# First-microsecond DMA order in a gated attention mix: two weight pieces on ScalarE's queue, and SyncE's later weights arranged around x

## Chip, core and metric

One core of one Trainium2 chip. The metric is the device time of one execution in microseconds (us), median of several runs. The time runs about 1.7 us above the profiled span. Differences in this study are a few tenths of a per cent, so most kernels were timed in five rounds next to the kernel before, on the same chip. "k=1" and so on is a quarter of the contraction dimension (2 of 8 tiles of 128 rows). "Half 0" and "half 1" are two sets of 512 output columns.

## The reference, cut to what matters

```python
def reference(A_x, A_wqkv, A_wo, B_x, B_wqkv, B_wo, gate_w):
    x = A_x                                            # [1, 2048, 1024] bf16
    g = sigmoid((x * gate_w).sum(-1, keepdims=True))
    a = A_ref(x, A_wqkv, A_wo)                         # linear attention, 32 heads
    b = B_ref(x, B_wqkv, B_wo)                         # sliding window, dilated, softmax
    return g * a + (1 - g) * b
# inside A_ref (cut): qkv = x @ wqkv; q, k, v = split(qkv); pk = phi(k)
```

The change touches only the start of the first stage, `k = x @ wqkv[:, D:2D]` of block A.

## The kernel before

TensorE first runs 34 small warm-up matmuls on a tile of ones. It then computes K for four blocks of 128 rows at once, one quarter of the contraction after the other, in eight PSUM banks (the memory that TensorE adds up in). It can start when the first x piece (transposed by the DMA) and the first weight piece have landed.

```python
    load_wk(nc.scalar, 0, 0)              # weights of quarter k=0, half 0: ScalarE's queue
    with tc.manual_schedule(engines={SP}):
        load_xT(0, 0, 2)                  # x, k=0, row blocks 0 and 1 (transposing DMA, L94)
        load_xT(0, 2, 4)                  # x, k=0, row blocks 2 and 3
        load_wk(nc.sync, 0, 1)            # weights, k=0, half 1 (L98, 256 KB)
        for k in range(1, 4):
            load_xT(k, 0, 4)
            load_wk(nc.sync, k, 0)
            load_wk(nc.sync, k, 1)
        for t in range(4, NB):            # then the rest of x, row block by row block
            nc.sync.dma_start_transpose(out=xT[:, :, t * P:(t + 1) * P], ...)
    ...                                   # cut
            warm_up(34)
            first = [bank_k(i) for i in range(8)]
            for k in range(4):
                for half in range(2):
                    for t in range(4):
                        for kt in (2 * k, 2 * k + 1):
                            project(first[4 * half + t], t, kt, half)   # L168
                        if k == 3:
                            phi(work, pk[:, t, half * 512:(half + 1) * 512], first[4 * half + t])
            # then t = 4 .. 15; then the G stage (L219), and all the rest
```

## Time and profile before

| | kernel before |
|---|---|
| median before the prediction (3 runs) | 474.15 us (474.14 to 475.01) |
| median with 3 more runs, taken beside the changed kernel | 474.49 us (474.14 to 475.10) |
| the profiled run itself | 475.14 us, span 473.4 us |
| first K matmul / 17th (first of k=1) / first of G | 4.74 / 10.33 / 62.1 us |

The profile's table of busy time, one line: busy us, share of the span, instructions.

```profile
...
PE 466.0 (98%) x5731; PEld 244.6 (52%) x5762; DVE 277.7 (59%) x602; ACT 169.0 (36%) x272; POOL 15.3 (3%) x30
...
```

After the first ten microseconds TensorE's list of waits has nothing over 0.2 us. The waits in the whole run (us in total, times, longest):

```profile
PE pk_ps L168 <- DMA WkA<-in_A_wqkv_dram: 1.5, 1, 1.5
PE warm L174 <- DVE onesb L165: 1.1, 1, 1.1
...
```

The chain of work that ended last, in order of time (start, duration, what), shows which piece that wait is for. It is the weight DMA that SyncE issued at 5.36 us, and matmuls run from 10.33 us on.

```profile
...
4.07 1.24 SPq L94
5.32 0.05 issue
5.36 4.93 DMA WkA<-in_A_wqkv_dram
10.29 0.04 issue
10.33 1.67 PE pk_ps L168 x7
...
```

The next view gives the busy time of the K matmuls alone in stretches of 2 us. The columns are: stretch, its length, busy time and (x) how many matmuls lie in it or reach into it, granted clock, DMA share, GB/s. At full rate a stretch counts 11 (one start per 0.216 us, plus those that reach over its edges), at low clock 6. Some records are missing from a trace: here the 16th matmul's, due at 8.69 us.

```profile
4.00:6.00 2.00, 1.26 (x4) 1.00 0.83 170
6.00:8.00 2.00, 2.00 (x10) 1.00 1.15 227
8.00:10.00 2.00, 0.85 (x4) 1.00 1.50 227
10.00:12.00 2.00, 1.67 (x8) 1.00 0.79 178
```

The stretch from 8 to 10 us is half empty: that is the wait. The first four matmuls start 0.40 to 0.43 us apart and the rest 0.216 us apart. The full clock is recorded from 6.20 us. The clock column (the 1.00 before the DMA share) doesn't show that; only the spacing does.

### The profile page before, as it was taken

What the parts mean: (1) busy time and instruction counts of PE and PEld (TensorE: products, weight loads), DVE (VectorE), ACT (ScalarE), POOL (GpSimd) and SP (SyncE); (2) the same over time, 40 slices, a digit from 0 to 9 for tenths busy, and PEclk for the clock granted to TensorE, in tenths of its full rate; (3) what the DMA queues carried; (4) which work ended last, traced back from release to release, by engine and by line L of the source; (5) the groups of instructions that cost most, each with busy time, mean ns of one, the idle gap of its engine ahead of it and who ended that gap; (6) DMA issues with size and microseconds to landing.
All of it is one profiled execution on the core that took longest, in us unless ns stands there. A gap on an engine that the chain in (4) does not pass through costs nothing.

```text
span 473.4 us, 13138 instructions
## 1 busy us (share of the span) xinstructions
PE 466.0 (98%) x5731; PEld 244.6 (52%) x5762; DVE 277.7 (59%) x602; ACT 169.0 (36%) x272; POOL 15.3 (3%) x30
## 2 busy tenths in 40 slices
PE   7999999999999999999999999999999999999997
PEld 5444444444444444445666666666664444444444
DVE  0496689991329999999567676767560049800000
ACT  1343321102443333333555555555551134221122
POOL 2300000500000000000000000000000000000000
PEclk9999999999999999999999999999999999999999
DMA  8999980000644233627327455442663923221111
GB/s 168 231 225 381 349 269 0 0 1 0 204 133 111 96 137 126 161 96 241 106 57 101 81 85 94 102 91 51 91 167 73 200 90 78 68 55 45 35 34 45
DMA packets 98780, 55.40 MB, mean 117 GB/s; under 512 B 70178, under 2 KB 90658, under 8 KB 98722
## 3 DMA queue, kind: packets, MB, share of 16 engines
q1 hardware_dynamic: 93554, 50.10, 42.3%
q10 hardware_dynamic: 5168, 4.46, 2.9%
q8 instruction: 45, 0.74, 0.7%
q14 instruction: 13, 0.11, 0.1%
HBM read 26.10 MB, written 15.86 MB: 89 GB/s over the span
## 4 chain that ended last, share of the span: by engine, by line
PE 97%; DMA 1%; SPq 1%; issue 0%; ACT 0%
PE q_ps L387 26%; PE d_ps L584 12%; PE p_ps L294 12%; PE g_ps L219 12%; PE e_ps L584 11%; PE pk_ps L168 11%; PE p_ps L330 9%; PE po L466 2%; PE s2b L444 2%; DMA WkA<-in_A_wqkv_dram 1%; SPq L94 1%; PE kv_ps L239 0%; PE w_ps L282 0%; SPq L98 0%; ACT osb L589 0%
## 5 line engine op out<-in xcount | busy, mean ns | idle before, releaser
L387 PE MATMUL q_ps<-xT,WqB 64*64 64x512 bf16 x1024 | 68.3, 377 | 0.0
L387 PE MATMUL q_ps<-xT,WkB 64*64 64x512 bf16 x1024 | 67.9, 377 | 0.0
L153 DVE TENSOR_SCALAR e<-e 128x512 f32<-128x512 f32 x64 | 27.1, 423 | 64.5 <-ACT e L152 64.5
L294 PE MATMUL p_ps<-WvB,xT 128*128 128x512 bf16 x250 | 57.3, 379 | 0.5 <-issue 0.3
L168 PE MATMUL pk_ps<-WkA,xT 128*128 128x512 bf16 x251 | 55.9, 383 | 1.7 <-DMA WkA<-in_A_wqkv_dram 1.5
L219 PE MATMUL g_ps<-pk,xrow 128*128 128x512 bf16 x251 | 55.2, 379 | 0.3
L449 ACT ACTIVATE PT<-s2b 128x928 bf16<-128x928 f32 (+4 forms) x40 | 34.1, 854 | 45.6 <-PE s2b L444 45.6
L451 DVE TENSOR_TENSOR PT<-PT,mask 128x928 bf16<-128x928 bf16 (+4 forms) x40 | 23.6, 590 | 37.8 <-ACT PT L449 37.8
L330 PE MATMUL p_ps<-WqA,xT 128*128 128x512 bf16 x187 | 43.1, 379 | 0.3
L168 PEld LDWEIGHTS <-xT 128*128 128x128 bf16 x256 | 25.1, 99 | 32.0 <-issue 2.5
L584 PEld LDWEIGHTS <-pqT 128*128 128x128 bf16 x272 | 26.0, 98 | 29.8 <-issue 0.4
L584 PEld LDWEIGHTS <-OBT 128*128 128x128 bf16 x272 | 26.0, 98 | 29.4
L219 PEld LDWEIGHTS <-xrow 128*128 128x128 bf16 x256 | 25.1, 98 | 30.2
L294 PEld LDWEIGHTS <-xT 128*128 128x128 bf16 x256 | 24.6, 98 | 30.0 <-issue 0.9
L387 PEld LDWEIGHTS <-WkB 64*64 64x64 bf16 x1024 | 31.8, 107 | 15.4 <-issue 0.4
L387 PEld LDWEIGHTS <-WqB 64*64 64x64 bf16 x1024 | 31.5, 106 | 15.5 <-issue 0.9
L152 ACT ACTIVATE e<-pk_ps 128x512 f32<-128x512 f32 x32 | 18.9, 597 | 42.0 <-PE pk_ps L168 36.6
L299 ACT CAST tmp<-p_ps 128x512 bf16<-128x512 f32 x32 | 18.7, 589 | 37.6 <-PE p_ps L294 31.2
L584 PE MATMUL d_ps<-WoA,pqT 128*128 128x512 bf16 (+1 forms) x133 | 30.7, 370 | 0.2
L584 PE MATMUL d_ps<-WoB,OBT 128*128 128x512 bf16 (+1 forms) x134 | 30.7, 370 | 0.1
L330 PEld LDWEIGHTS <-xT 128*128 128x128 bf16 x192 | 18.8, 98 | 22.7
L584 PE MATMUL e_ps<-WoB,OBT 128*128 128x512 bf16 (+2 forms) x133 | 29.7, 363 | 0.2
(62 smaller groups left out, 484.1 us busy)
## 6 DMA issues: line engine op xcount, KB each, us to landing
vd<-tmp SPq DMA_DIRECT2D x16, 264.0 KB
xrow<-in_A_x_dram SPq DMA_DIRECT2D x4, 1024.0 KB
out_dram<-osb ACTq DMA_DIRECT2D x31, 128.0 KB
pqd<-tmp SPq DMA_DIRECT2D x12, 256.0 KB
WvA<-in_A_wqkv_dram SPq DMA_DIRECT2D x2, 1024.0 KB
WoA<-in_A_wo_dram SPq DMA_DIRECT2D x2, 1024.0 KB
WvB<-in_B_wqkv_dram SPq DMA_DIRECT2D x2, 1024.0 KB
WqA<-in_A_wqkv_dram SPq DMA_DIRECT2D x2, 1024.0 KB
```

What stands on the lines that cost most here:

```text
L152: nc.scalar.activation(out=e[:], in_=pj[:], func=ACT.Exp)
L153: nc.vector.tensor_scalar(out=e[:], in0=e[:], scalar1=1.0, scalar2=1e-6, op0=ALU.min, op1=ALU.add)
L168: nc.tensor.matmul(pj[:], lhsT=xT[:, kt, t * P:(t + 1) * P], rhs=WkA[half][:, kt, :], start=(kt == 0), stop=(kt == KT - 1))
L219: nc.tensor.matmul(pj[:], lhsT=xrow[:, t, kt * P:(kt + 1) * P], rhs=pk[:, t, half * 512:(half + 1) * 512], start=(t == 0), stop=(t == NB - 1))
L294: nc.tensor.matmul(st["pj"][:], lhsT=xT[:, kt, t * P:(t + 1) * P], rhs=WvB[half][:, kt, :], start=(kt == 0), stop=(kt == KT - 1))
L299: nc.scalar.copy(out=v[:, half * 16:(half + 1) * 16, 0:Dh], in_=st["pj"][:].rearrange("p (h e) -> p h e", h=16))
L330: nc.tensor.matmul(st["pj"][:], lhsT=xT[:, kt, t * P:(t + 1) * P], rhs=WqA[half][:, kt, :], start=(kt == 0), stop=(kt == KT - 1))
L387: nc.tensor.matmul(banks[o][64 * j:64 * j + 64, :], lhsT=lhsT(r, kt, j), rhs=rhs(r, kt), start=first and kt == 0, stop=kt == KT - 1, skip_ ...
L444: nc.tensor.matmul(s2b[64 * par:64 * par + 64, pair, :, o:o + w], lhsT=kts[c][r, par, k0:k0 + 64], rhs=qz[r, :, par, q0 % 512:q0 % 512 + w ...
L449: nc.scalar.activation(out=pt[:, :, 0:W_], in_=s2b[:].rearrange("p a b s -> p (a b) s")[:, :, 0:W_], func=ACT.Exp, scale=SCALE)
L451: nc.vector.tensor_tensor(out=pt[:, :, 0:W_], in0=pt[:, :, 0:W_], in1=mask[:, None, base:base + W_].broadcast_to([P, 4, W_]), op=ALU.mult)
L584: nc.tensor.matmul(st["ps"][:, 0:n], lhsT=lhsT, rhs=W[c0 // 512][:, c, c0 % 512:c0 % 512 + n], start=(side == 0 and c == 0), stop=(side == ...
```

## The change

Its intent: take one 256 KB weight piece off SyncE's queue in front of x of k=1, and put one of the two weight pieces of each later quarter ahead of its x piece, so that TensorE finds the second quarter ready.

```diff
     load_wk(nc.scalar, 0, 0)
+    load_wk(nc.scalar, 0, 1)
     with tc.manual_schedule(engines={SP}):
         load_xT(0, 0, 2)
         load_xT(0, 2, 4)
-        load_wk(nc.sync, 0, 1)
         for k in range(1, 4):
+            load_wk(nc.sync, k, 0)
             load_xT(k, 0, 4)
-            load_wk(nc.sync, k, 0)
             load_wk(nc.sync, k, 1)
```

The instruction streams of TensorE, VectorE and GpSimd are the same in both kernels. ScalarE has one DMA issue more, SyncE one less.

## The prediction

> **What bounds the kernel now.** TensorE. The profile's busy table gives PE 466.0 of 473.4 us (98%), and the chain of waits is 97% PE. PE's waits list has one DMA wait in the run: 1.5 us for WkA. The timeline shows where it is: the first matmul of the K projection starts at 4.74 us, the 16 matmuls of the first quarter (k=0) are done issuing by 8.7 us, and the next one starts at 10.33 us. From there PE runs at 0.216 us a matmul nearly without a gap to the end. So a microsecond won before 10.33 us should be one of the total; PE, DVE and POOL streams are unchanged.
>
> **What the change does.** A SyncE weight issue takes 0.47 to 0.60 us, an x transpose 1.23 to 1.3 us. By the trace's semaphore updates, pieces on SyncE's queue land in issue order: slot 3 (issued 3.44) at 6.98, slot 4 (4.07, x of k=1) at 7.99, slot 5 (5.36) at 10.29, slot 6 (5.98) at 11.01, slot 7 (6.50, x of k=2) at 12.06, slots 8, 9 at 12.84, 13.56, slot 10 (x of k=3) at 14.54, slots 11, 12 at 15.30, 16.02. Before, slot 5 was the weights of k=1, half 0: PE waits for it until 10.29. After, these weights sit in slot 3 (6.98), and slot 5 is k=1, half 1. The x pieces of k=1 to 3 keep their slots.
>
> If the slots land as before, PE needs: k=1 at 8.7 (weights 6.98, x 7.99: no wait); k=1 half 1 at 10.4 (slot 5, 10.29: just in time); k=2 at 12.15 (x 12.06: just in time); k=3 at 15.6 (x 14.54). So at most 10.33 - 8.70 = 1.6 us is won.
>
> **What it costs.** k=0 half 1 moves to ScalarE's queue, issued at about 1.3 us, so its 256 KB (about 0.75 us of 16 engines at 47 ns a 1 KB packet) flow beside the first x piece, which lands at 4.70 and starts PE. The Trainium skill ("DMA: Bandwidth & Descriptors", "Issuing engines are not separate DMA queues") says that both queues run on the same 16 engines and interleave. The windows view gives a DMA share of 0.73 to 0.88 from 2 to 5 us, so some room; I estimate the first matmul is late by 0.2 to 0.5 us. Part is given back: PE runs at 0.43 us a matmul until 6.2 us, where the full clock is granted, so a late start loses only slow matmuls.
>
> Net gain about 1.3 us (0.3%).
>
> **Predicted time: 472.8 us**, 472.0 to 474.0 (8 in 10). Faster by over 2%: 0.01; within 2%: 0.98; slower by over 2%: 0.01.
>
> **What would show each step.** Right: PE's 1.5 us wait for WkA is gone or below 0.5 us; the first K matmul starts at 4.9 to 5.3 us; the 17th starts near 8.9 to 9.3 us; the G stage starts about 1.3 us earlier than 62.29; later stages keep their lengths. Wrong: a new wait of similar size at k=1 half 1, at x of k=2, or at the first x piece.
>
> **What would make it wrong.** Transposes of x stalling for over 1 us (256-byte packets begun at 9.24 us ended near 10.87) at another place, now where PE has no slack; the granted clock rising later because PE pauses between the warm-up matmuls and the first real one; run-to-run spread (474.14 to 475.01), which is as large as the gain.

## More of the kernel before

("Slow run" further down is this document's own word for a run over 475 us.)

## The result, and the profile after

| | before | after |
|---|---|---|
| median, 6 runs each | 474.49 us | 473.87 us |
| range | 474.14 to 475.10 | 473.68 to 474.32 |
| first K matmul / 17th / first of G | 4.74 / 10.33 / 62.1 us | 5.62 / 9.08 / 60.9 us |

The ratio of the fast runs is 0.9988, with a 95% interval from 0.9975 to 1.0000. It is the mean time of one kernel's fast runs over that of the other's of the same rounds, so not quite the ratio of the medians. The interval just reaches 1: this set alone hardly shows a gain.

TensorE's waits after. The wait for weights is gone, and another has come in front of the very first matmul:

```profile
PE warm L174 <- DVE onesb L165: 1.1, 1, 1.1
PE pk_ps L168 <- DMA xT<-in_A_x_dram: 0.8, 1, 0.8
```

The chain after. The first x piece, issued at 0.80 us as before, now reports its landing only at 5.57 us, and no other DMA is in the chain up to 12 us:

```profile
...
0.80 4.77 DMA xT<-in_A_x_dram
5.57 0.04 issue
5.62 6.43 PE pk_ps L168 x29
```

The same stretches as before, for the K matmuls alone. The first stretch has nearly none, then the rate is full without a hole:

```profile
4.00:6.00 2.00, 0.39 (x2) 1.00 1.02 249
6.00:8.00 2.00, 2.00 (x11) 1.00 1.07 227
8.00:10.00 2.00, 2.00 (x11) 1.00 1.15 234
10.00:12.00 2.00, 2.00 (x11) 1.00 0.93 226
```

In these two profiles the difference is accounted for. Before, the first 16 matmuls took 5.59 us (10.33 - 4.74): 16 x 0.216 = 3.45 us of work, 0.71 us because the first four ran at low clock, and 1.43 us of waiting. After, they took 3.46 us. So 2.13 us are won and 0.88 us lost at the start, a net of 1.25 us. This is what the start of G shows (62.13 to 60.88), and from there to the end both runs take the same time (411.24 us). It is twice the difference of the medians: the profiled run of before was one of its slowest (475.14 us). The profiled run of after was an ordinary one (473.85 us), in which the full clock came early, at 4.48 us.

Landing times, read from the updates of each DMA's semaphore (the counter by which it reports) in the two traces (the last of its 16):

| piece on SyncE's queue | before: content, landed | after: content, landed |
|---|---|---|
| 1 | x k=0 blocks 0, 1: 4.70 | same: 5.57 |
| 2 | x k=0 blocks 2, 3: 5.30 | same: 5.94 |
| 3 | weights k=0 half 1: 6.98 | weights k=1 half 0: 7.04 |
| 4 | x k=1: 7.99 | x k=1: 7.96 |
| 5 | weights k=1 half 0: 10.29 | weights k=1 half 1: 10.07 |
| 6 | weights k=1 half 1: 11.01 | weights k=2 half 0: 10.77 |
| 7 | x k=2: 12.06 | x k=2: 11.84 |

In these two traces a place, from the third on, keeps its landing time within 0.25 us though another piece stands in it. Only the first two x pieces are later. Other traces are less regular: in four profiles with the DMA order of after, the fifth place landed between 9.44 and 10.13 us.

Why the first x piece is later can be seen in the DMA packets. The counts are per 0.1 us, taken from the packet records of the trace of after. q1 is SyncE's queue, q10 ScalarE's. The first x piece is 512 packets of 256 bytes. After each piece come 32 packets of 4 bytes, which I take for its report of completion:

```
from us   q1 256 B   q1 4 B   q10 1 KB
3.6          41         0         6
3.7          28         0        23
3.8          16         0        28
3.9           1         0        33
4.0           0         0        33
4.1           0         0        36
4.2           0         0        36
4.3           0         0        39
4.4          42        26         9
4.5          88         4         2
```

All 512 data packets of the first x piece have started by 3.9 us. From 4.0 to 4.4 us no packet of SyncE's queue starts, neither its completion packets nor the data of the second x piece. The second weight piece on ScalarE's queue has the engines to itself. When that piece is through, the completions follow. In the trace of before, with no such piece, they ran from 3.2 to 3.6 us. All six profiles with this piece issued at 1.30 us have the gap, of 0.52 us, begun at 3.66 to 3.91 us; those with no second piece on ScalarE's queue by then have none.

The Trainium skill ("DMA: Bandwidth & Descriptors", "Queues, rings and completion order") says that each engine takes turns between the queues that have work for it, and that a completion write lands only after all earlier writes of that engine, across queues. It adds that a turn lasts a whole packet in the page's own sense, typically 9 to 17 descriptors. An estimate: the weight piece is 256 transfers of 1 KB, 16 for each of 16 engines, and the trace has 0.046 us for one, so a single turn could hold 0.74 us of it. A gap of 0.52 us is within what this allows. But it isn't the whole: in the three kernels further down that hold the piece back to 2.29 us, SyncE's queue also starts nothing for 0.28 to 0.81 us, just after the first x piece has sent its 4-byte packets, while only 20 to 45 packets of ScalarE's piece start and on average 6 to 9 of the 16 engines are busy with them. The ordered completion write could account for the completions being late, but the second x piece's data stood still as well. The runs show the gap, not which rule makes it.

### The profile page after: what moved, and what is told of

Read it like the earlier page. It is cut to its first block, busy times and chain, and to the rows that moved or that the text cites. A ratio compares the mean times of both kernels' runs of the same rounds, so it can differ in the third digit from the quotient of the medians.

```text
span 472.1 us, 13169 instructions
## 1 busy us (share of the span) xinstructions
PE 467.1 (99%) x5762; PEld 244.3 (52%) x5762; DVE 277.8 (59%) x602; ACT 169.0 (36%) x272; POOL 15.4 (3%) x30
## 3 DMA queue, kind: packets, MB, share of 16 engines
q10 hardware_dynamic: 5440, 4.72, 3.1%
## 4 chain that ended last, share of the span: by engine, by line
PE 98%; DMA 1%; ACT 0%; issue 0%
PE q_ps L387 27%; PE d_ps L584 12%; PE p_ps L294 12%; PE pk_ps L168 12%; PE g_ps L219 12%; PE e_ps L584 12%; PE p_ps L330 9%; PE po L466 2%; PE s2b L444 2%; DMA xT<-in_A_x_dram 1%; PE kv_ps L239 0%; PE w_ps L282 0%; ACT osb L589 0%
## 5 line engine op out<-in xcount | busy, mean ns | idle before, releaser
L387 PE MATMUL q_ps<-xT,WqB 64*64 64x512 bf16 x1024 | 68.3, 377 | 0.0
L387 PE MATMUL q_ps<-xT,WkB 64*64 64x512 bf16 x1024 | 67.9, 377 | 0.0
L584 PEld LDWEIGHTS <-pqT 128*128 128x128 bf16 x272 | 26.0, 98 | 29.7 <-issue 0.4
L584 PEld LDWEIGHTS <-OBT 128*128 128x128 bf16 x272 | 26.0, 98 | 29.4
L387 PEld LDWEIGHTS <-WkB 64*64 64x64 bf16 x1024 | 31.7, 107 | 15.4 <-issue 0.4
L387 PEld LDWEIGHTS <-WqB 64*64 64x64 bf16 x1024 | 31.5, 106 | 15.6 <-issue 0.9
L584 PE MATMUL d_ps<-WoA,pqT 128*128 128x512 bf16 (+1 forms) x136 | 30.9, 370 | 0.0
L584 PE MATMUL d_ps<-WoB,OBT 128*128 128x512 bf16 (+1 forms) x136 | 30.8, 370 | 0.0
L584 PE MATMUL e_ps<-WoA,pqT 128*128 128x512 bf16 (+2 forms) x136 | 30.0, 363 | 0.0
```

The costliest lines, as they stand in the source:

```text
L387: nc.tensor.matmul(banks[o][64 * j:64 * j + 64, :], lhsT=lhsT(r, kt, j), rhs=rhs(r, kt), start=first and kt == 0, stop=kt == KT - 1, skip_ ...
L584: nc.tensor.matmul(st["ps"][:, 0:n], lhsT=lhsT, rhs=W[c0 // 512][:, c, c0 % 512:c0 % 512 + n], start=(side == 0 and c == 0), stop=(side == ...
```

## Experiments

Theory at the start: the gain is the removed wait, and the late first x piece is the price of the piece moved to ScalarE's queue. Rivals: the new arrangement around x is what helps; the lateness was chance or came from the order of issue. Twelve runs were made, of nine further kernels and three repeats, and all gave correct results. The medians of the kernel before, on the chips of the three sets, were 474.85, 474.82 and 474.93 us.

### The changed kernel again

No edit.

> The changed kernel once more, as the measure for the other runs and a second profile. My theory: the first K matmul waits for the first x piece again, starting at 5.2 to 5.7 us (4.74 in the profile of before), no wait for weights; the time at which the full clock is granted differs from run to run (6.2 us in the profile of before, 4.5 us in that of after), and G starts at 60.9 to 61.6 us. Median 473.9 us. Rival (the late first x piece was chance): the first matmul starts at 4.7 to 4.9 us.

Measured: median 474.73 us (473.65 to 476.29), ratio 0.9998 (0.9981 to 1.0014). The first matmul started at 5.82 us, so the late first x piece was no chance. But three of six runs took over 475 us. The profile is of the slowest one (476.29 us), and the same view of the K matmuls in stretches shows why:

```profile
4.00:6.00 2.00, 0.18 (x1) 1.00 1.03 227
6.00:8.00 2.00, 2.00 (x6) 1.00 1.10 247
8.00:10.00 2.00, 2.00 (x6) 1.00 1.25 251
10.00:12.00 2.00, 1.95 (x9) 1.00 1.00 261
```

Six matmuls in 2 us where the first profile had eleven: the array ran at low clock until 10.39 us, where the full clock is recorded. G started at 63.3 us, later than before. This was not foreseen in size: I had expected a clock that differs between 4.5 and 6.2 us.

The Trainium skill ("TensorE: Matmul & The Clock Gate", Part 1) says that the clock is raised after a busy activity window of about 3.4 us, and that this window runs freely, so that its phase differs from run to run. The 10.39 us fit this: one window earlier, 6.98 us, closes a window (3.57 to 6.98) in which TensorE had paused for 0.90 us between the last warm-up matmul and the first real one. That pause is new: in the kernel before, the warm-up led straight into the first matmul.

### The rearrangement alone

```diff
         load_xT(0, 2, 4)
+        load_wk(nc.sync, 0, 1)        # back on SyncE's queue (and off ScalarE's)
         for k in range(1, 4):
             load_wk(nc.sync, k, 0)    # as in the change
```

> Half 1 of the first weight quarter goes back to SyncE's queue, just after the first x pieces; the later weights stay arranged around their x piece. My theory: what counts is that one 256 KB piece leaves SyncE's queue, so here the first matmul starts at 4.7 us as before, but the x piece of k=1 is now the fifth piece of the queue and lands at 9.3 to 10.3 us, so that PE waits about 1 us for it: G starts at 61.6 to 62.2 us, median 474.4 us, as before. Rival (the arrangement of weights around x makes the gain): no such wait, 473.9 us or less.

Measured: median 474.19 us (473.84 to 474.54), ratio 0.9984 (0.9972 to 0.9996). The first matmul started at 4.63 us, as expected, and TensorE's waits in its profile were these (the warm-up's left out):

```profile
...
PE pk_ps L168 <- DMA xT<-in_A_x_dram: 0.8, 1, 0.8
...
PE pk_ps L168 <- DMA WkA<-in_A_wqkv_dram: 0.3, 1, 0.3
```

The wait for x of k=1 (landed 9.23 us) is there, as my theory said. Still, the time is better than before, against my number, and G started at 61.09 us, where I had expected 61.6 to 62.2. That is as early as in the two profiles of the changed kernel's faster runs (60.88 and 61.11 us). In both orders TensorE can start k=1 when the fifth piece of SyncE's queue has landed: here that is x, at 9.23 us; before it is a weight piece behind x, at 10.2 to 10.3 us in two profiles. Why the fifth place is sooner in this order isn't settled. One difference: in both profiles of before, x packets of 256 bytes begun from 9.2 us on stalled for over 1 us and ended at 10.8 to 10.9 us (the prediction names this), while here no packet begun before 12.8 us took over 0.6 us. One profile doesn't show whether that is the order's doing. In any case the rearrangement alone reached most of the gain, so my theory that only the piece leaving SyncE's queue counts did not hold.

### The move alone

```diff
         for k in range(1, 4):
-            load_wk(nc.sync, k, 0)
             load_xT(k, 0, 4)
+            load_wk(nc.sync, k, 0)
             load_wk(nc.sync, k, 1)
```

(relative to the changed kernel)

> Half 1 of the first quarter on ScalarE's queue as in the change, but SyncE issues x, then both weights of each later quarter, as before. My theory: the x piece of k=1 lands near 7.4 us, its weights near 8.0 us, PE has no wait for weights, the first x piece is late as after (first matmul 5.2 to 5.7 us), and the median is within 0.2 us of the changed kernel's, 473.9 us. Rival (the arrangement makes the gain): PE waits for the weights of k=1 past 9 us, 474.4 us.

Measured: median 474.03 us; six runs, four from 473.67 to 474.12 us, and two of 476.21 and 476.35 us. The ratio is 0.9995 (0.9976 to 1.0013). The profile, of a fast run, has one DMA wait, of 0.9 us, for the first x piece. The 17th matmul starts at 8.92 us without one listed, but only just: the weights of k=1 landed at 8.88 us, not at the 8.0 us that I expected. G started at 60.72 us. So the arrangement adds little once the piece is moved, and the slow runs came with the move: this kernel pauses 0.91 us before its first matmul as well, and the kernel with the rearrangement alone, which doesn't pause, had no run over 474.54 us.

### Holding the piece back: a first try

Three VectorE memsets of the tile's first quarter come ahead of the DMA that writes it, and the issue is moved down in the program to follow them.

```diff
-    load_wk(nc.scalar, 0, 1)
...
-            nc.vector.memset(onesb[:], 1.0)
+            nc.vector.memset(onesb[:], 1.0)
+            nc.vector.memset(WkA[1][:, 0:2, :], 0.0)    # three times
+            load_wk(nc.scalar, 0, 1)
```

> The changed kernel, with the issue of the second weight piece on ScalarE's queue held back from 1.3 us to about 2.8 us by three VectorE memsets of the tile that it writes. My theory: its packets then no longer run before the first x piece reports its landing; the first matmul starts at 4.7 to 4.9 us, the piece itself lands by 6.6 us, PE waits under 0.3 us for it, G starts at 60.0 to 60.9 us, and the median is 0.4 to 0.8 us below the changed kernel's. Rival (the first x piece is late for another reason, such as the order of issue on SyncE): the first matmul stays at 5.5 us and the time at 473.9 us.

Measured: 478.44 us, 0.7% slower than before (1.0056 to 1.0082). This was not the experiment I meant. The memsets ended at 2.92 us, but being later in the program, the DMA had been given the semaphore of the first x piece, and so was issued only after that had landed, at 4.56 us. The piece landed at 10.05 us. The longest of TensorE's waits in this profile is for it:

```profile
PE pk_ps L168 <- DMA WkA<-in_A_wqkv_dram: 2.3, 1, 2.3
...
```

It still taught two things. With nothing of ScalarE's queue behind the first weight piece, the first x piece landed at 4.48 us. And the pause of 2.3 us cost the clock: the records show it full from 7.10 us, half from 10.52 to 13.93 us, then full again, in steps of 3.41 us, which agrees with the skill's window.

### A longer warm-up

```diff
-            warm_up(34)
+            warm_up(44)
```

(relative to the changed kernel)

> The changed kernel with 44 warm-up matmuls in place of 34 (0.107 us each while the clock is low), so that TensorE is not idle for 0.9 us before the first x piece lands at 5.6 to 5.8 us. Theory: it is this pause that, in some runs, puts off the full clock by one window (10.4 us in the second profile of the changed kernel, against 4.5 in the first). Then no run is slow here: the full clock comes before 7.6 us in the profile, all runs lie within 473.4 to 474.5 us, median about 473.8 us, against 473.7 to 476.3 us with 34. Rival (the late clock comes from something else[...]): runs over 475 us stay, about one in four.

Measured: median 474.87 us (473.76 to 475.07), ratio 0.9994 (0.9980 to 1.0008). No run is in the 476 range, and the pause is gone from the profile, where the full clock is recorded at 6.91 us. But my range was wrong: three of five runs lie at 474.87 to 475.07 us. The profile (475.0 us) shows what I left out. The warm-up ran until the first matmul at 5.79 us, 0.3 us past the landing of the x piece (5.47), and a start at 5.79 with full clock at 6.91 leaves three slow matmuls. G started at 61.60 us, 0.72 us after the first profile of the changed kernel; another 0.40 us was lost after that, in a stage that is the same in all kernels (see "Why the prediction was right or wrong"). The longer warm-up gained no time here. One run of five, at 475.07 us, is over the 475 us of the rival, and five runs are too few to show that the slow ones are gone.

### The pause without the change

The kernel before, with a shorter warm-up:

```diff
-            warm_up(34)
+            warm_up(26)
```

> The kernel before with 26 warm-up matmuls in place of 34: TensorE idles from about 3.9 us to the first x piece at 4.7 us, a pause of 0.8 us without any of the change. Theory (the pause puts off the clock in some runs): some of the runs are slow by 1 to 2 us, over 476 us, where the full clock comes after 8 us; the others stay at 474.3 to 475.3 us. Rival (the pause costs nothing): all runs are as those of the kernel before, 474.3 to 475.4 us.

Measured: median 475.37 us (474.80 to 475.90), ratio 1.0012 (1.0000 to 1.0025). In the profile TensorE pauses 0.71 us before the first x piece, the full clock comes at 8.68 us, and the K matmuls run at half rate until then, as the view in stretches shows:

```profile
4.00:6.00 2.00, 1.22 (x3) 1.00 0.77 176
6.00:8.00 2.00, 2.00 (x6) 1.00 1.23 204
8.00:10.00 2.00, 2.00 (x9) 1.00 1.63 243
```

So in this profile the clock comes late after a pause, without any of the change. But the cost that I expected, over 476 us, did not come. The slow first matmuls filled the time in which the kernel before would have waited anyway: the 17th started at 10.43 us, 0.10 us after the 10.33 us of the profile of before, and G at 62.22 us, 0.09 us later. The removed wait had been a cushion.

### A double dose on ScalarE's queue

```diff
-    load_wk(nc.scalar, 0, 1)
+    load_wk(nc.scalar, 0, 1); load_wk(nc.scalar, 1, 0)    # and not on SyncE's queue
```

> A double dose: ScalarE's queue issues the first weights of k=1 (half 0) as well, right after the two pieces of the first quarter, and SyncE has one piece less before x of k=1. Theory (packets of ScalarE's queue put off the landing of the x pieces): the first x piece lands another 0.3 to 0.9 us later, at 5.9 to 6.5 us, the first matmul starts there, and the pause of TensorE grows to 1.2 to 1.8 us, so that most runs get the full clock late: median 474.5 to 476 us. Rival (the delay came from the order of issue alone): first matmul at 5.6 us as in the changed kernel.

Measured: median 474.40 us (474.20 to 474.56), ratio 0.9992 (0.9980 to 1.0005). My number for the first x piece was wrong: it landed at 5.80 us, as in the changed kernel (5.57 to 5.80 in its three profiles). The second x piece paid instead, landing at 6.80 us in place of 5.94 to 6.16. So more on ScalarE's queue did not delay the first x piece further. It fits better that an x piece is held up by the ScalarE piece that is moving when it would report: the third piece landed at 6.46 us, 0.34 us before the second x piece. The first matmul started at 5.85 us after a pause of 0.95 us, but no run was slow (the clock came at 4.75 us in the profiled one); my expectation of mostly slow runs failed.

### Holding the piece back, properly

```diff
-    load_wk(nc.scalar, 0, 1)
+    nc.vector.memset(WkA[1][:, 0:2, :], 0.0); nc.vector.memset(WkA[1][:, 0:2, :], 0.0)
+    load_wk(nc.scalar, 0, 1)
```

(in its old place in the program, so that it has a semaphore of its own)

> Again the changed kernel with the second weight piece on ScalarE's queue held back, now by two memsets of VectorE alone (in the run before, the piece had also got the semaphore of the first x piece, and so was issued only after that had landed, at 4.56 us). It is issued at about 2.3 us here in place of 1.3 us. Theory: the first x piece lands at 4.6 to 5.2 us in place of 5.6, since fewer of the piece's packets run before it reports; the first matmul starts by 5.2 us, a pause of under 0.6 us; the piece lands by 6.3 us; the wait for it is under 0.3 us; median 0 to 0.5 us below the changed kernel's fast runs (473.3 to 473.9 us). Rival: the first x piece lands at 5.5 us or later all the same.

Measured: median 474.09 us (473.74 to 474.42), ratio 0.9985 (0.9972 to 0.9997). The piece was issued at 2.29 us. The first x piece landed at 4.20 us, better than expected, and the first matmul started at 4.72 us without a pause. The piece landed at 6.11 us, and the *second* x piece right after it, at 6.54 us. TensorE's waits in this profile, the warm-up's left out:

```profile
...
PE pk_ps L168 <- DMA xT<-in_A_x_dram: 0.4, 1, 0.4
...
```

The chain of work that ended last now runs through the second x piece, issued at 2.15 us:

```profile
...
2.15 4.39 DMA xT<-in_A_x_dram
6.54 0.05 issue
6.59 2.55 PE pk_ps L168 x11
...
```

This confirms the cause by moving it: issue the ScalarE piece at 1.30 us and it is the first x piece that reports right after it (0.27 to 0.37 us after, in five profiles; 0.64 in the double dose); issue it at 2.29 us and it is the second, 0.43 to 0.45 us after it (this profile and the next two). One thing stays unexplained: the first x piece landed at 4.06 to 4.35 us in these three profiles, sooner than in those with no second piece on ScalarE's queue by then (4.48 to 4.74 us).

### Held back, with the matmuls in the order of landing

```diff
             for k in range(4):
+                for pair in ((0, 1), (2, 3)) if k == 0 else ((0, 1, 2, 3),):
                     for half in range(2):
-                        for t in range(4):
+                        for t in pair:
```

(relative to the kernel just above; one more run has 31 warm-up matmuls in place of 34)

> The kernel of the last set in which the second weight piece is issued at 2.3 us, and in which TensorE waited 0.4 us for the second x piece (landed 6.54, the weight piece 6.11). Here the matmuls of the first quarter are taken in another order: row blocks 0 and 1 with both halves of the weights, then row blocks 2 and 3, so that the weight piece is needed first and the second x piece after eight matmuls. Theory: that wait of 0.4 us goes, the second half of the quarter is done by 8.8 us or earlier, G starts at 60.4 to 60.9 us, the median is 0.2 to 0.5 us below that of the kernel before it (474.1), so 473.6 to 473.9, with no run over 474.6. Rival (the first microseconds are pinned by the landing of the next quarter, as in the kernel before): no gain, a new wait before the 17th matmul.

> The same with 31 warm-up matmuls in place of 34: in the last profile the first x piece had landed at 4.2 us, but TensorE was in the warm-up until 4.7. Theory: the first matmul starts at 4.4 to 4.7 us with no pause over 0.3 us, and the gain is 0 to 0.3 us beside 34 warm-ups. Rival (even a short pause puts off the full clock): one run or more slower by over 1 us.

Measured with 34: median 473.83 us (473.53 to 474.27), ratio 0.9976 (0.9964 to 0.9988). With 31: 473.68 us (473.39 to 474.12), ratio 0.9973 (0.9961 to 0.9985). The first matmul starts at 4.46 and 4.40 us. The wait for x is gone, but its place is taken by a wait for the weight piece, which I had not expected. From TensorE's waits in the profile with 31 warm-ups:

```profile
...
PE pk_ps L168 <- DMA WkA<-in_A_wqkv_dram: 0.5, 1, 0.5
...
```

With 34 it is 0.8 us, since the clock came at 4.17 us there and the first four matmuls were done sooner. The start of G, at 60.65 us with 34, lies where I expected it. The difference between the two warm-ups, and that to the kernel one step before, lie within their intervals. Both are faster than the kernel before: their intervals end at 0.9988 and 0.9985.

### The changed kernel a third time, and the kernel before a second profile

> The changed kernel a third time, beside the others of this set: it tells whether its slow runs come back (three of twelve so far took over 475 us). Theory: one or two of the five or six take over 475 us[...]; the rest 473.6 to 474.4. The first matmul starts at 5.4 to 5.9 us.

Measured: median 474.03 us (473.55 to 476.37), ratio 0.9987 (0.9969 to 1.0004), one slow run in six. The first matmul started at 5.84 us. The clock had been full since 3.80 us, and stayed so over a pause of 1.4 us.

> The kernel before, for a second profile: the only profile of it is of one of its slowest runs (475.14 us; median 474.5 to 474.9). Theory: the wait of TensorE for the first weights of k=1 ends at 9.7 to 10.4 us whatever the time of the full clock, G starts at 61.5 to 62.2 us.

Measured: one run of 475.04 us (state unknown). Here the array was at full rate from the first matmul on (4.66 us, starts 0.22 us apart), and it gained nothing. TensorE's waits in this run:

```profile
PE pk_ps L168 <- DMA WkA<-in_A_wqkv_dram: 2.0, 2, 1.6
...
```

And its chain of work that ended last, in order of time:

```profile
...
5.37 4.84 DMA WkA<-in_A_wqkv_dram
10.21 0.04 issue
10.25 1.89 PE pk_ps L168 x8
...
```

The same piece lands at 10.21 us (10.29 in the first profile), and G starts at 62.05 us (62.13). What the clock gave in the first quarter went into a longer wait. In these two runs the time of the kernel before is set by that landing, not by the clock.

### Pause and clock in all profiles

| kernel | pause before the first K matmul, us | full clock from, us |
|---|---|---|
| before | none | 6.20 |
| rearrangement alone | none | 4.46 |
| held back, first try | none | 7.10 |
| longer warm-up | none | 6.91 |
| held back; pairs; pairs with 31 | none | 5.62; 4.17; 5.52 |
| after, three profiles | 0.84; 0.90; 1.39 | 4.48; 10.39; 3.80 |
| move alone | 0.91 | 3.91 |
| double dose | 0.95 | 4.75 |
| before, 26 warm-ups | 0.71 | 8.68 |

The second profile of before is left out, since it has no clock record. The pauses are counted from the modelled end of the last warm-up matmul, as the view of waits does; counted from its start plus one spacing they are 0.16 to 0.21 us longer (0.91 us in the last row). Without a pause the clock comes anywhere from 4.2 to 7.1 us. With one it either comes before the first matmul (by 4.75 us) or after 8.6 us, and nothing lies between. The slow runs of the changed kernel are 4 of 18 (475.08 to 476.37 us), those with the move alone 2 of 6. The mark of 475 us was set by eye: the kernel before passes it in 12 of 37 runs, but never goes over 475.43 us. Only one of the slow runs was profiled (476.29 us), so that the others have the same cause is inferred from it, not seen.

## Why the prediction was right or wrong

The predicted time was 472.8 us (472.0 to 474.0); 473.87 us were measured. The class "within 2%" and the range held. The predicted gain of 1.35 us (474.15 to 472.8) was twice the 0.62 us between the medians.

- **What bounds the kernel: right.** TensorE is busy throughout, and the only DMA wait is the one at 10.33 us. A shift there was a shift of the whole run: 1.25 us at the start of G, and 1.3 us in the span (473.4 to 472.1).
- **The wait for WkA goes: right.** It isn't in any profile of the changed kernel. The places on SyncE's queue from the third on landed within 0.25 us of before in the first profile, and no new wait came at k=1 half 1 (10.07 us, needed at 10.80) or at x of k=2.
- **"I estimate the first matmul is late by 0.2 to 0.5 us": the step that failed.** It was late by 0.88, 1.08 and 1.10 us in the three profiles. I read the free DMA share as room to share. The traces show instead that SyncE's queue stood still for 0.52 us while the second weight piece moved, and an x piece whose data was through reported only after it.
- **"A late start loses only slow matmuls": wrong in some runs.** The pause that comes with the late start can put off the full clock by a whole window, as the second profile shows. I had named this as a risk without a weight.
- **The base: too low.** The three runs gave 474.15 us, six gave 474.49, and those of the later sets 474.8 to 474.9. The one profile was of a run of 475.14 us. I took a median from one run and the 1.5 us of wait from another. Why the runs of before differ by over 1 us among themselves isn't settled: in two profiles with quite different clocks G starts within 0.1 us. Both are of runs over 475 us. An estimate for the fastest run of before: 474.14 us less 1.72 us beside the span and 411.24 us after the start of G leaves 61.2 us for the start of G, so its wait may have been some 0.9 us shorter than the profiled one; no such run was profiled. Part of the spread lies elsewhere: from the start of G to the end the profiles take 411.14 to 411.73 us, and the difference is in the attention stage (first L387 to first L584 matmul, 141.18 to 141.76 us), which no edit touched. The start of G therefore tells more of the change than one run's time.
- **The size as a whole.** The agreement of the span (1.3 us) with the prediction is partly luck: the start was later than I put it (0.88 against 0.2 to 0.5 us), and the clock in that run came earlier (4.48 against 6.20 us), which saved the 0.71 us of slow matmuls. Over three sets, the 14 of 18 runs that weren't slow average 473.9 us, against 474.8 us for all 37 runs of before (474.14 to 475.43): 0.9 us, a sum that leaves out the worst runs on one side only. The four slow ones take half of that back (mean of all 18: 474.4 us).
- **The change as a bundle.** In the experiments I first gave the gain to the piece that leaves SyncE's queue. But G starts at 61.09 us with the rearrangement alone and at 60.72 us with the move alone (one profile each), against 60.88 and 61.11 us with both: either half does it, and they don't add up.

So where did the expected gain go? The old wait was 1.5 us of weights in the profiled run, and probably less in the faster runs of before. Of these 1.5 us, 0.9 to 1.1 came back as a first x piece that reports late, and now and then more is lost, in the one slow run that was profiled because the array starts with its clock low. The version that holds the piece back and takes the matmuls in the order of landing keeps the gain (473.68 us, ratio 0.9973 to before). The 15 runs of the three kernels that hold it back to 2.29 us had no slow one (all up to 474.42 us). In the last set the mean with 31 warm-ups is 0.6 us below that of the changed kernel, and most of that is the changed kernel's one slow run.

## What to carry to other kernels

At a cold start, ask not only how soon a transfer is issued but which transfer will be moving when the one that everybody waits for has to report its landing; a second queue can help the later pieces and hold up the first. If a kernel warms TensorE up before its data arrives, a change that moves the landing can open a pause in which the clock may come late; look at the warm-up again, but note that here making it longer closed the pause and gained no time. A wait that ends at a fixed time hides every loss and every gain in front of it, so take it out of the sum before judging what comes earlier.

## What the Trainium skill lacked or had wrong

- "DMA: Bandwidth & Descriptors", "Issuing engines are not separate DMA queues": it says that queues interleave; only another section ("Queues, rings and completion order") gives the grain, a whole packet at a time. What neither draws out is the consequence: SyncE's queue started no packet for 0.52 us while a 256 KB piece of ScalarE's queue moved (six profiles), and the x piece in flight reported 0.27 to 0.64 us after that piece (nine profiles). Nor does either explain a queue that stands still for 0.28 to 0.81 us while on average 6 to 9 of 16 engines are busy with the other.
- "TensorE: Matmul & The Clock Gate", Part 1: the free-running window of 3.4 us agrees (steps of 3.41 us in one trace). What is lacking is how much idle time a window may hold. Here windows are counted back from the recorded rise, and idle time runs from a matmul's start plus one spacing to the next start. A window with 0.73 us of idle at its start (0.39 to 3.80 us, third profile of the changed kernel) still raised the clock; one with 0.84 us at its start (0.28 to 3.69 us, held back, first try), one with a pause of 0.91 us (1.86 to 5.27 us, 26 warm-ups) and one with 1.10 us (3.57 to 6.98 us) did not. So in these four traces the limit lies between 0.73 and 0.84 us. For the drop, a window with 2.46 us of idle (7.10 to 10.52 us, held back, first try) sufficed, and one with 1.56 us (3.80 to 7.21 us, third profile) did not. The page's advice for modelling, that the ramp costs under 1%, is true here too (up to 2.5 us of 474), but it was as large as the whole gain under study.
- The same page warns that clock records can't be fully trusted: agreed. One profile had no record at all, though its matmuls started 0.22 us apart from the beginning.
